# Rows of y and the blocks for the checks issued from GpSimd's queue instead of SyncE's, in a PEER + FNet kernel

## The chip, the core and the metric

The kernel runs on one core of one Trainium2 chip. The metric is the device time of one execution in microseconds (us), the median over several runs of the same program; lower is better.

## What is computed

The reference adds three things for x of 2048 rows by 512 columns, with xn the layer norm of x:

```python
def _A_ref(x, dft_seq_re, dft_seq_im, dft_hid_re, dft_hid_im):   # FNet: real part of a 2-D DFT
    a = jnp.einsum("bsd,ed->bse", x, dft_hid_re)
    b = jnp.einsum("bsd,ed->bse", x, dft_hid_im)
    return jnp.einsum("ts,bse->bte", dft_seq_re, a) - jnp.einsum("ts,bse->bte", dft_seq_im, b)
...
    # PEER: 32 heads, 64 + 64 half keys, top 2 of each half, top 2 of the 4 pairs, 4096 experts
    q = jnp.einsum("nd,dhc->nhc", xf, w_q)
    s1 = jnp.einsum("nhd,ed->nhe", q1, k1)
    s2 = jnp.einsum("nhd,ed->nhe", q2, k2)
...
    g = _softmax(top_s, axis=-1)
    act = _gelu(jnp.einsum("nd,nhkd->nhk", xf, u[top_e]))
    out = jnp.einsum("nhk,nhk,nhkd->nd", g, act, v[top_e])
...
    return x + _A_ref(xn, ...) + _B_ref(xn, ...)
```

## The kernel before

The work has two phases. The first, up to some 440 us, computes the DFT part and the scores s1 and s2 with the choice of the top experts; the DFT part goes to memory as `y_d`, one row of 128 x 512 for each of the 16 blocks of 128 rows. The second phase, which the change touches, doesn't gather experts. For each block b it computes z = x u for all 4096 experts ("z"), applies gelu, multiplies by a gate matrix that holds g at the chosen experts and zero elsewhere, and multiplies the product by v ("v").

The phases stand in a list (lines 1540 to 1543): z of blocks 0 and 1, v of block 0, and then seven times z of a pair (b, b+1), v of the odd block b-1 and v of the even block b; v of block 15 ends it. I call z, v(odd), v(even) a round. In a v block (`v_part`, line 1330) 16 groups of v are multiplied one after the other. Nine of the groups lie in SBUF; the others are loaded from `v_d` (512 KB each) into a ring of three places (`v_load`, line 1306), each load as soon as TensorE has finished with the place.

The gate matrices are made beside this, in quarters. `g_mm(b, k)`: VectorE builds two one-hot matrices L (line 1260) and R (lines 1265, 1268) in a ring of three pairs, and TensorE multiplies them (line 1270). `w_part(b, k)`: VectorE multiplies the result by the activations into a tile w (line 1278), ScalarE copies it to 16 bits (line 1285), and VectorE takes the remainder (line 1286). A table (lines 1544 to 1615) puts them between the eight steps of a v block. In even blocks 2 to 12 it says (lines 1570 to 1580)

```python
put(ph, 1, G(b + 1, 0))
put(ph, 3, G(b + 1, 1))
put(ph, 5, W(b + 1, 0))
put(ph, 7, W(b + 1, 1), G(b + 1, 2))
```

so that TensorE's instructions for G(b+1, 2) stand right behind the last v matmul of the even block and ahead of the next z phase.

The kernel also tests whether its inputs are what its shortcuts assume. `compare` (from line 1350) loads a piece of C (`ca`, 64 KB, line 1357, and `cb`, 448 KB, line 1358) into a tile cx, VectorE reduces and subtracts (lines 1359, 1378, 1384), and ScalarE sums what is left (line 1404). `fit` loads pieces of wq (512 KB, line 1455) or v (256 KB, line 1462), and ScalarE sums them. All of these and the w tiles share four buffers (`WB`, tag "w"). The same table gives them steps: the checks of C run in z phases and in both kinds of v block.

The row of the output: `add_x(b)` loads y of the block from `y_d` (line 1340) and adds x to it with an accumulating transfer from GpSimd (line 1341); `finish(b)` adds the v product on VectorE (line 1345) and stores y (line 1346). y has one buffer, so the load for b+1 waits until the store for b has landed. For block 15 y is loaded earlier, and lines 1312 to 1322 add and store it in halves.

Every transfer is issued by an engine's own queue, in program order: SyncE's queue (SP) for all of the above but line 1341, GpSimd's (POOL) for line 1341. Where one of them waits, for a buffer or a landing, everything behind it in the same queue waits too. A scheduler arranges each engine's instructions and adds the waits. A second program (`safe`) stands behind a branch; it isn't executed on these inputs.

Of the kernel before, what the change touches and what calls it, by code (L numbers as in the profile page):

```python
# [18 lines left out]
P = 128  # L19
S = 2048  # L20
D = 512
KD = D // P
NT = S // P
# [7 lines left out]
V2 = 9  # L31
# [5 lines left out]
def tile_fnet_peer(ctx, tc, x, ca, cb, c5, wt, wf, wr, wq, kt, ut, vn, out):  # L37
# [9 lines left out]
    nc = tc.nc  # L47

    dram = ctx.enter_context(tc.tile_pool(name="dram", bufs=1, space=bass.MemoryType.DRAM))
    y_d = dram.tile([NT, P, D], F32, name="y_d")  # L50
    xt_d = dram.tile([NT, P, 2 * KD * P], F16, name="xt_d")
    z_d = dram.tile([NT, P, 3 * P], F16, name="z_d")
    v_d = dram.tile([16 - V2, P, 4 * D], F16, name="v_d")
# [667 lines left out]
    def part_b(safe, stS, stP, stQ, stE, xt, u_sb, cmp_p, w4):  # L721
# [615 lines left out]

        def add_x(b):
            Y[b] = y = bp.tile([P, D], F32, tag="y", name=f"y{b}", bufs=1)
            nc.sync.dma_start(y, y_d[b])  # L1340
            nc.gpsimd.dma_start(y, x[b % 4, b // 4], accum_op=ALU.add)  # L1341

        def finish(b, pv):
            y = Y[b]
            nc.vector.scalar_tensor_tensor(y, pv, osc, y, op0=ALU.mult, op1=ALU.add)
            nc.sync.dma_start(out[b * P:(b + 1) * P], y)

        later = []

        def compare(n):  # L1350

            ri, g, kk = n // 32, n // 8 % 4, n % 8
            odd = kk // 4
            t = bp.tile([P, 4, 4, 64], F32, tag="w", name=f"cx{n}", bufs=WB)
            tf = t.rearrange("p s q c -> p (s q c)")
            tv = t.rearrange("p s q c -> p s (q c)")
            nc.sync.dma_start(tf[:, :P], ca[ri, g, :, kk * P:(kk + 1) * P])
            nc.sync.dma_start(tf[:, P:], cb[ri, g, kk].rearrange("p b c -> p (b c)"))
            nc.vector.tensor_reduce(asum[:, n:n + 1], tf[:, :P], axis=AX.X, op=ALU.add,
                                    apply_absolute_value=True)  # L1360
            sgn = (((1, 1, 1), (-1, 1, -1)), ((-1, -1, 1), (1, -1, -1)))[ri][odd]
            ops = [ALU.subtract if v > 0 else ALU.add for v in sgn]
            op = ops[1]
            if g == 0:
                nc.vector.tensor_tensor(tv[:, 1], tv[:, 1], tv[:, 0], op=ops[0])
                for i in (2, 3):
                    nc.vector.scalar_tensor_tensor(tv[:, i], tv[:, 0], not0, tv[:, i], op0=ALU.mult, op1=ops[i - 1])
                f = (-1 if ri else 1) * sgn[1] * sgn[2]
                nc.vector.tensor_tensor(tv[0:1, 3], tv[0:1, 3], tv[0:1, 2],
                                        op=ALU.subtract if f > 0 else ALU.add)  # L1370
            else:
                sets = {}
                for i, o in enumerate(ops):
                    sets.setdefault(o, []).append(i + 1)
                for o, ix in sets.items():
                    sl = slice(ix[0], ix[-1] + 1, ix[1] - ix[0] if len(ix) > 1 else 1)
                    v = tv[:, sl]
                    nc.vector.tensor_tensor(v, v, tv[:, 0:1].to_broadcast([P, len(ix), 256]), op=o)
            m = ALU.add if ri else ALU.subtract

            def mirror(v):

                c = 0 if kk else 1
                nc.vector.tensor_tensor(v[:, 2:4, c:], v[:, 2:4, c:], v[:, 0:2, c:], op=m)  # L1384
                if c:
                    nc.vector.tensor_tensor(v[:, 3, 0:1], v[:, 3, 0:1], v[:, 2, 0:1], op=m)

            if g == 0:
                mirror(t[0:1, 2])
                if odd and ri:  # L1390

                    nc.vector.tensor_copy(t[0:1, 2, 0:2], t[0:1, 0, 0:2])
                elif odd == ri:
                    if ri:
                        nc.vector.memset(t[0:1, 2, 0:2], 0.0)
                    else:
                        v = t[0:1, 2, 0:2].rearrange("p q (c a) -> p (q c) a", a=2)
                        nc.vector.tensor_tensor(v, v, c52.unsqueeze(1).to_broadcast([1, 64, 2]), op=ALU.add)
                    if kk == 0:
                        nc.vector.memset(t[0:1, 2, 2, 0:1], 0.0)  # L1400
            mirror(t[:, 0])
            if kk == 0:
                nc.vector.memset(t[:, 0, 2, 0:1], 0.0)
            later.append(lambda: nc.scalar.activation(tf[:, P:], tf[:, P:], AF.Abs, accum_out=chk[:, n:n + 1]))  # L1404
# [46 lines left out]
        def fit(n):  # L1451

            if n < NK:
                t = bp.tile([P, 2 * D], F32, tag="w", name=f"fit{n}", bufs=WB)
                nc.sync.dma_start(t.rearrange("p (h k) -> p h k", h=2), wq[1 + n // 4, n % 4 // 2, n % 2])
                later.append(lambda: nc.scalar.activation(t, t, AF.Abs, accum_out=fits[:, n:n + 1]))
                return
            g = n - NW
            t = bp.tile([P, 2 * D], F32, tag="w", name=f"fit{n}", bufs=WB)
            if g >= 16 + V2:  # L1460
                h = t.bitcast(F16)[:, 0:2 * D]
                nc.sync.dma_start(h, v_d[g - 16 - V2, :, 0:2 * D])
                later.append(lambda: nc.scalar.activation(h, h, AF.Abs, accum_out=fits[:, n:n + 1]))
                return
            src = (u_sb[g][:, 0].rearrange("p c k e -> p (c k e)") if g < 16 else
                   v_sb[g - 16][:, 0].rearrange("p c d -> p (c d)"))
            nc.scalar.activation(t, src, AF.Abs, accum_out=fits[:, n:n + 1])

        def verdict():
# [35 lines left out]
            nc.vector.tensor_tensor(flags, flag, flag2, op=ALU.max)  # L1505

        fit_units = [iter([lambda n=n: fit(n) for n in ns]) for ns in (
            (*range(NK), *range(NW + 16 + V2, NW + 32)), range(NW, NW + 16 + V2))]
        units = iter([lambda n=n: (compare if n < 64 else compare_w)(n) for n in range(68)])
# [106 lines left out]
        for n, ph in enumerate(phases):  # L1616
            if ph[0] == "z":
                b = ph[1:]
# [13 lines left out]
            b = ph[1]  # L1632
# [8 lines left out]
            for cg in range(8):  # L1641
                v_part(b, pv, cg)
                for f in plan.get((ph, cg), ()):
                    f()
                if b + 1 == NT and cg == 3 and not safe:
                    step(None)
                    add_x(b)
                    verdict()
            if b + 1 < NT or safe:
                add_x(b)  # L1650
            else:
                ret = nc.values_load(flags, min_val=0, max_val=1)
            if b + 1 < NT or safe:
                finish(b, pv)
# [30 lines left out]
    with tc.If(rv > 0):  # L1685
        with tc.tile_pool(name="gen", bufs=1) as gp, \
# [4 lines left out]
            def gsplit(src, shape, tag, name, scale=1.0, bufs=2):  # L1691
                h = gp.tile(shape, F32R, tag=tag + "h", name=name + "h", bufs=bufs)
                l = gp.tile(shape, F32R, tag=tag + "l", name=name + "l", bufs=bufs)
                nc.scalar.activation(h, src, AF.Copy, scale=scale)
                nc.vector.scalar_tensor_tensor(l, src, scale, h.bitcast(F32), op0=ALU.mult,
                                               op1=ALU.subtract)
                return h, l

            def gload(src, shape, tag, name):
                t = gp.tile(shape, F32, tag=tag, name=name, bufs=2)  # L1700
                nc.sync.dma_start(t, src)
                return t

            gx = []
            for i in range(NT):
                t = gload(x[i % 4, i // 4], [P, D], "x", f"gx{i}")
                norm(t, t, i)
                gx.append(gsplit(t, [P, D], "xs", f"gxs{i}", 1.0 / XS, NT))
            for q in range(4):
                ya = gp.tile([P, 4, D], F32, tag="ya", name=f"gya{q}")  # L1710
                for ri in range(2):
                    pp = [gps.tile([P, 512], F32, tag="gp", name=f"gp{q}{ri}{d}", bufs=4)
                          for d in range(KD)]
                    for i in range(NT):
                        t = gp.tile([P, 512], F32, tag="c", name=f"gc{q}{ri}{i}", bufs=2)
                        g, sq = divmod(i, 4)
# [4 lines left out]
                        h, l = gsplit(t, [P, 512], "cs", f"gcs{q}{ri}{i}")  # L1721
# [9 lines left out]
                    for kd, pieces in enumerate((((0, 1, P, 0), (P - 1, 0, 1, 2)), ((0, 1, P, 1), (P - 1, 0, 1, 0)),  # L1731
                                                 ((0, 0, 1, 1), (1, 1, P, 2)), ((0, 0, P, 3),))):
                        t = gp.tile([P, 512], F32, tag="c", name=f"gw{q}{ri}{kd}", bufs=2)
# [3 lines left out]
                    for a in range(4):  # L1737
                        py = pb(f"gy{q}{ri}{a}")
                        n = 0
# [9 lines left out]
                        b = 4 * a + q  # L1749
                        o = gload(out[b * P:(b + 1) * P], [P, D], "o", f"go{b}")  # L1750
                        y = gload(y_d[b], [P, D], "y", f"gy{b}")
# [53 lines left out]
```

## Time and profile before

| | |
|---|---|
| median of 3 runs | 1126.24 us (1125.17 to 1126.28) |
| the profiled execution | 1128.96 us, of which the span from first to last instruction is 1127.1 |
| granted TensorE clock, mean | 0.997 of full speed |
| busy share of the span: TensorE, VectorE, ScalarE, GpSimd | 98%, 85%, 59%, 28% |
| transfers issued from SP's kind of queue | 200.65 MB |
| transfers issued from GpSimd's queue | 4.20 MB |

A profile shows one execution. Engines are PE (TensorE matmul), PEld (its weight loads), DVE (VectorE), ACT (ScalarE), POOL (GpSimd) and SP (SyncE; SPq is its queue of transfers). L1340 is line 1340 of the kernel. In a timeline row the first number is the start in us, the second the duration; xN says how many equal instructions the row joins, and brackets tell how long the engine was idle before it and what ended that. A row of waits gives who waited, for whom, the total in us, how often, and the longest.

### The profile page before, as it was taken

What the parts mean: (1) busy time and instruction counts of PE and PEld (TensorE: products, weight loads), DVE (VectorE), ACT (ScalarE), POOL (GpSimd) and SP (SyncE); (2) the same over time, 40 slices, a digit from 0 to 9 for tenths busy, and PEclk for the clock granted to TensorE, in tenths of its full rate; (3) what the DMA queues carried; (4) which work ended last, traced back from release to release, by engine and by line L of the source; (5) the groups of instructions that cost most, each with busy time, mean ns of one, the idle gap of its engine ahead of it and who ended that gap; (6) DMA issues with size and microseconds to landing.
All of it is one profiled execution on the core that took longest, in us unless ns stands there. A gap on an engine that the chain in (4) does not pass through costs nothing.

```text
span 1127.1 us, 27990 instructions
## 1 busy us (share of the span) xinstructions
PE 1109.9 (98%) x11024; PEld 719.9 (64%) x11024; DVE 957.2 (85%) x2883; ACT 668.5 (59%) x1118; POOL 314.6 (28%) x365
## 2 busy tenths in 40 slices
PE   9999999999999999999999999999999999999997
PEld 6455554544545459788488479479469569559643
DVE  7899989989889899976996987987997887878882
ACT  6557698798898465465446546535545635545541
POOL 1515998888889750000000000000000000000000
PEclk9999999999999999999999999999999999999999
DMA  9884455356353315773764764864765765656263
GB/s 296 270 215 163 162 180 204 116 157 200 94 185 105 102 52 186 211 233 121 266 206 156 254 191 162 262 194 146 261 199 167 246 188 191 225 197 189 94 179 116
DMA packets 123932, 206.80 MB, mean 183 GB/s; under 512 B 34564, under 2 KB 65419, under 8 KB 123790
## 3 DMA queue, kind: packets, MB, share of 16 engines
q1 hardware_dynamic: 121184, 200.65, 54.7%
q0 software_dynamic: 2304, 4.20, 2.4%
q8 instruction: 88, 1.44, 0.5%
q14 instruction: 54, 0.44, 0.1%
q10 hardware_dynamic: 302, 0.08, 0.0%
HBM read 171.52 MB, written 27.59 MB: 177 GB/s over the span
## 4 chain that ended last, share of the span: by engine, by line
PE 45%; DVE 12%; DMA 6%; ACT 2%; POOL 2%; issue 1%; SPq 0%; ACTq 0%; POOLq 0%; DVEq 0%
PE z L1173 16%; PE v L1330 16%; PE z L1095 9%; PE g L1270 3%; DMA v<-v_d 2%; DVE L L1260 2%; DMA cx<-in_cb_dram 2%; DVE w L1278 2%; DVE vals L956 1%; DMA fit<-in_wq_dram 1%; DVE idx L960 1%; DVE act L1286 1%; DVE R L1268 1%; DVE R L1265 1%; DVE w L1286 1%
## 5 line engine op out<-in xcount | busy, mean ns | idle before, releaser
L252 PE MATMUL s<-m,xq 128*128 128x512 f16 x1344 | 297.4, 379 | 0.6 <-ACT ss L952 0.5
L1330 PE MATMUL v<-v,act 128*128 128x512 f16 x1044 | 231.1, 379 | 1.9 <-DMA v<-v_d 1.9
L252 PEld LDWEIGHTS <-xq 128*128 128x128 f16 x1344 | 129.7, 98 | 151.8 <-issue 2.0
L1341 POOL DMA_DIRECT2D y<-in_x_dram x16 | 14.4, 897 | 652.9 <-DMA y<-y_d 219.0
L1260 DVE TENSOR_TENSOR L<-io_lam,cmp 128x2048 f16<-128x2048 f16 x128 | 156.0, 1218 | 31.5 <-PE g L1270 31.5
L1330 PEld LDWEIGHTS <-act 128*128 128x128 f16 x1044 | 100.0, 98 | 118.5 <-issue 2.7
L956 DVE MAX8 vals<-ss 128x8 f32<-128x64 f32 x896 | 133.4, 216 | 3.9 <-ACT ss L952 3.9
L1095 PE MATMUL z<-xb,u 128*128 128x128 f16 (+1 forms) x1440 | 121.8, 244 | 0.1
L1173 PEld LDWEIGHTS <-u 128*128 128x128 f16 x2016 | 114.5, 98 | 1.1 <-issue 0.8
L1095 PEld LDWEIGHTS <-u 128*128 128x128 f16 x1440 | 107.6, 98 | 7.4 <-issue 0.2
L1330 PE MATMUL v<-v,w 128*128 128x512 f16 x480 | 106.7, 379 | 0.7 <-DMA v<-v_d 0.6
L952 ACT ACTIVATE ss<-s,wsc 128x512 f32<-128x512 f32 x120 | 81.3, 682 | 38.7 <-PE s L252 33.4
L1404 ACT ACTIVATE cx<-cx 128x896 f32<-128x896 f32 x64 | 60.5, 946 | 64.2 <-DVE cx L1384 34.4
L960 DVE FIND_INDEX8 idx<-vals,ss 128x8 uint16<-128x256 f32 x224 | 93.7, 418 | 0.0
L1173 PEld LDWEIGHTS <-s 128*128 128x128 f16 x1440 | 82.5, 98 | 0.2
L1330 PEld LDWEIGHTS <-w 128*128 128x128 f16 x480 | 46.0, 98 | 54.5 <-issue 1.6
L1285 ACT ACTIVATE act<-w 128x1024 f16<-128x1024 f32 x36 | 48.3, 1356 | 53.7 <-DVE w L1278 53.3
L1270 PEld LDWEIGHTS <-L 128*128 128x128 f16 x2048 | 60.5, 96 | 13.1 <-issue 2.4
L1278 DVE SCALAR_TENSOR_TENSOR w<-act,scl,g 128x1024 f32<-128x1024 f32 x44 | 55.8, 1277 | 10.6 <-ACT act L1203 10.3
L1270 PE MATMUL g<-R,L 128*128 128x32 f16 x2048 | 61.9, 176 | 1.9 <-DVE R L1268 1.8
L1173 PE MATMUL z<-xb,u 128*128 128x128 f16 x1008 | 63.1, 219 | 0.0
L1286 DVE TENSOR_TENSOR act<-w,act 128x1024 f16<-128x1024 f32 x44 | 58.5, 1329 | 3.8 <-ACT act L1285 3.7
(366 smaller groups left out, 1855.7 us busy)
## 6 DMA issues: line engine op xcount, KB each, us to landing
v<-v_d SPq DMA_DIRECT2D x67, 512.0 KB, 5.5
cx<-in_cb_dram SPq DMA_DIRECT2D x64, 448.0 KB, 5.0
s<-s_d SPq DMA_DIRECT2D x42, 512.0 KB, 4.3
w<-in_wq_dram SPq DMA_DIRECT2D x28, 512.0 KB, 6.5
fit<-in_wq_dram SPq DMA_DIRECT2D x28, 512.0 KB, 3.8
uv<-in_vn_dram SPq DMA_DIRECT2D x16, 512.0 KB, 3.8
uv<-in_ut_dram SPq DMA_DIRECT2D x16, 512.0 KB, 3.9
s_d<-v SPq DMA_DIRECT2D x24, 256.0 KB, 4.2
```

The lines of the kernel that those rows point to most:

```text
L252: nc.tensor.matmul(ps, xt[i][:, l, kd, :], m[:, r, kd, :], start=(n == 0), stop=(n == 3 * KD - 1))
L952: nc.scalar.activation(s, ps, AF.Copy, scale=inv)
L956: nc.vector.max(vals[:, i, w, :, h], s[:, g, :])
L960: nc.vector.max_index(idx[:, i, w].rearrange("p k h -> p (k h)"), vals[:, i, w, 0:2].rearrange("p k h -> p (k h)"), s[:, w * HC:g + 1, :]. ...
L1095: nc.tensor.matmul(ps if n == 1 else ps.rearrange("p (b n) -> p b n", b=2), ug[:, l, c % 2, kd, :], xb2[:, k0, r, kd, :] if n == 1 else xb ...
L1173: nc.tensor.matmul(bank[:, t * P:(t + 1) * P], lt, rt, start=(t == k == 0 and op in "125"), stop=(t == 3 and k == 5), skip_group_check=op ...
L1260: nc.vector.tensor_tensor(L.rearrange("p t (l two) -> p t l two", two=2), io_lam.rearrange("p (l two) -> p l two", two=2).unsqueeze(1).to_ ...
L1270: nc.tensor.matmul(p[:, hf, t * NC:(t + 1) * NC], L[:, t, :], R[:, t, :], start=True, stop=True)
L1278: nc.vector.scalar_tensor_tensor(w, act[:, :, ts], fw, p.rearrange("p h (n c) -> p c (h n)", c=NC), op0=ALU.mult, op1=ALU.mult)
L1286: nc.vector.tensor_tensor(w16[..., 1], w, w16[..., 0], op=ALU.subtract)
L1330: nc.tensor.matmul(pv, w16[:, c, :, l], v_sb[g][:, r, cc, :], start=(n + cc == 0 and k == 0), stop=(n == end and cc == 1 and k == 2))
L1404: later.append(lambda: nc.scalar.activation(tf[:, P:], tf[:, P:], AF.Abs, accum_out=chk[:, n:n + 1]))
```

## The change

The load and the store of y, both loads of a check of C, and the loads of wq and v for `fit` are issued from GpSimd's queue. The load of y for block 15 and everything in `safe` that concerns y stay on SP. The loads of v in the ring, of the z phases and of the last checks (`compare_w`) stay on SP too.

```diff
         def add_x(b):
             Y[b] = y = bp.tile([P, D], F32, tag="y", name=f"y{b}", bufs=1)
-            nc.sync.dma_start(y, y_d[b])
+            (nc.sync if safe or b + 1 == NT else nc.gpsimd).dma_start(y, y_d[b])
             nc.gpsimd.dma_start(y, x[b % 4, b // 4], accum_op=ALU.add)
 
         def finish(b, pv):
             y = Y[b]
             nc.vector.scalar_tensor_tensor(y, pv, osc, y, op0=ALU.mult, op1=ALU.add)
-            nc.sync.dma_start(out[b * P:(b + 1) * P], y)
+            (nc.sync if safe else nc.gpsimd).dma_start(out[b * P:(b + 1) * P], y)
...
-            nc.sync.dma_start(tf[:, :P], ca[ri, g, :, kk * P:(kk + 1) * P])
-            nc.sync.dma_start(tf[:, P:], cb[ri, g, kk].rearrange("p b c -> p (b c)"))
+            nc.gpsimd.dma_start(tf[:, :P], ca[ri, g, :, kk * P:(kk + 1) * P])
+            nc.gpsimd.dma_start(tf[:, P:], cb[ri, g, kk].rearrange("p b c -> p (b c)"))
...
-                nc.sync.dma_start(t.rearrange("p (h k) -> p h k", h=2), wq[1 + n // 4, n % 4 // 2, n % 2])
+                nc.gpsimd.dma_start(t.rearrange("p (h k) -> p h k", h=2), wq[1 + n // 4, n % 4 // 2, n % 2])
...
-                nc.sync.dma_start(h, v_d[g - 16 - V2, :, 0:2 * D])
+                nc.gpsimd.dma_start(h, v_d[g - 16 - V2, :, 0:2 * D])
```

Now what stands on the queues at one place, the turn from the odd block 3 to the even block 4. First SP before the change, from the store of block 3's row (y3) to the store of block 4's (y4); v12 to v9 are groups of v for the ring, cx20 and cx21 the next two checks of C, fit11 a piece of wq; brackets name the semaphores waited for (DMAHW and DMASW are those of landed transfers).

```order
L1346 DMA out_0_dram<-y3_9454 128x512 [waits DMAHW5_49,DVE_49]
L1306 DMA v12_4_9475<-v_d_60 128x2048 [waits DMAHW6_49,PE_49]
L1340 DMA y4_9733<-y_d_57 128x512 [waits DMAHW7_49,DMAHW5_49]
L1306 DMA v11_4_9489<-v_d_60 128x2048 [waits DMAHW0_49,PE_49]
L1357 DMA cx20_9648<-in_ca_dram 128x128 [waits DMAHW1_49,Activation_49]
L1358 DMA cx20_9648<-in_cb_dram 128x896 [waits DMAHW2_49]
L1357 DMA cx21_9668<-in_ca_dram 128x128 [waits DMAHW3_49,Activation_49]
L1358 DMA cx21_9668<-in_cb_dram 128x896 [waits DMAHW4_49]
L1306 DMA v10_4_9553<-v_d_60 128x2048 [waits PE_49]
L1455 DMA fit11_9731<-in_wq_dram 128x1024 [waits DMAHW6_49,DVE_49]
L1306 DMA v9_4_9616<-v_d_60 128x2048 [waits DMAHW7_49,PE_49]
L1346 DMA out_0_dram<-y4_9733 128x512 [waits DMAHW0_49,DVE_49]
```

Behind this, only the four loads of v (v12, v11, v10, v9) are left on SP here. GpSimd's queue before held only the accumulates of line 1341. With the change it reads, at the same place:

```order
L1346 DMA out_0_dram<-y3_9454 128x512 [waits DMASW6_49,DVE_49]
L1340 DMA y4_9733<-y_d_57 128x512 [waits DMASW7_49,DMASW6_49]
L1341 DMA y4_9733<-in_x_dram 128x512 [waits DMASW7_49,DMASW0_49]
L1357 DMA cx20_9648<-in_ca_dram 128x128 [waits DMASW1_49,Activation_49]
L1358 DMA cx20_9648<-in_cb_dram 128x896 [waits DMASW2_49]
L1357 DMA cx21_9668<-in_ca_dram 128x128 [waits DMASW3_49,Activation_49]
L1358 DMA cx21_9668<-in_cb_dram 128x896 [waits DMASW4_49]
L1455 DMA fit11_9731<-in_wq_dram 128x1024 [waits DMASW5_49,DVE_49]
L1346 DMA out_0_dram<-y4_9733 128x512 [waits DVE_49]
```

The accumulate of line 1341 now stands in the same queue between y's load and the checks' loads. Even blocks 2 to 12 all have this sequence. In all, 193 issues move from SP to GpSimd; TensorE's order is the same. On VectorE, in the even block of the same place, the operations stand as they stood; with the change:

```order
L1286 TENSOR_TENSOR w4_126<-w5_0_9643,w4_126 128x32x32 [waits Activation_49]
L1359 TENSOR_REDUCE sums_87<-cx20_9648 128x1 [waits DMASW1_49]
L1378 TENSOR_TENSOR cx20_9648<-cx20_9648 128x2x256 [waits DMASW2_49]
L1378 TENSOR_TENSOR cx20_9648<-cx20_9648 128x256
L1359 TENSOR_REDUCE sums_87<-cx21_9668 128x1 [waits DMASW3_49]
L1384 TENSOR_TENSOR cx20_9648<-cx20_9648 128x128 [waits DVE_49]
L1278 SCALAR_TENSOR_TENSOR w5_1_9687<-w4_126,scl_93,g5_1_9561 128x1024 [waits PE_49]
L1378 TENSOR_TENSOR cx21_9668<-cx21_9668 128x2x256 [waits DMASW4_49]
L1378 TENSOR_TENSOR cx21_9668<-cx21_9668 128x256
L1265 TENSOR_TENSOR R2_5741<-io_c_73,cmp5_9369 128x512
L1384 TENSOR_TENSOR cx21_9668<-cx21_9668 128x128 [waits DVE_49]
L1286 TENSOR_TENSOR w4_126<-w5_1_9687,w4_126 128x32x32 [waits Activation_49]
```

Behind these twelve rows follow the rest of R2 and the L0 and R0 that TensorE's G(5, 2) takes at the end of block 4, and then y4. The check's operations moved nowhere here; only the semaphores they wait for are others (DMASW, those of GpSimd's transfers).

## The prediction, made before the change was run

> **What bounds the kernel now.** I read the page's span and busy rows first, then the table by stretches over one round of the second phase, then what TensorE waits for there, and last the four timelines of one even block.
>
> ```profile
> span 1127.1 us, 27990 instructions
> PE 1109.9 (98%) x11024; PEld 719.9 (64%) x11024; DVE 957.2 (85%) x2883; ACT 668.5 (59%) x1118; POOL 314.6 (28%) x365
> 573.00:661.00 88.00, 87.12 (x1068) 63.22 (x1065) 73.45 (x120) 45.92 (x76) 1.72 (x2) 1.00 0.64 206
> PE v L1330 <- DMA v<-v_d: 2.5, 5, 0.9
> PE g L1270 <- DVE R L1268: 1.8, 4, 0.7
> PE z L1173 <- ACT act L1226: 0.6, 1, 0.6
> ```
>
> TensorE is the bound: 98% of the span, and 87.12 of the 88.00 us of a round (one z phase and two v blocks; columns of the third row: length, then PE, PEld, DVE, ACT, POOL busy, granted clock, DMA share, GB/s). The last three rows are everything that it waits for from 420 us to the end (total, times, longest): 2.5 us for a v block from memory, 1.8 for a one-hot R that VectorE builds, 0.6 for ScalarE, together 4.9. So transfers arriving earlier can win 4.9 us at most, and only the 2.5 are SyncE's doing. GpSimd is nearly idle in the round (1.72 of 88 us), and VectorE, with 73 of 88, has some slack, but the next rows show that it has none at the place where TensorE comes for R. Here are the issue rows (median us from issue to landing, last column) and GpSimd's only work in this phase, the x accumulate:
>
> ```profile
> v<-v_d SPq DMA_DIRECT2D x67, 512.0 KB, 5.5
> cx<-in_cb_dram SPq DMA_DIRECT2D x64, 448.0 KB, 5.0
> y<-y_d SPq DMA_DIRECT2D x16, 256.0 KB, 2.7
> y<-in_x_dram POOLq DMA_DIRECT2D x16, 256.0 KB, 6.1
> out_dram<-y SPq DMA_DIRECT2D x15, 256.0 KB, 2.8
> L1340 SPq DMA_DIRECT2D y<-y_d x16: 319/320/572, 445.2 to 1102.1; - x16
> L1341 POOL DMA_DIRECT2D y<-in_x_dram x16: 856/867/1177, 453.9 to 1107.4; - x16
> 578.84 0.87 POOL L1341 DMA_DIRECT2D y<-in_x_dram  x1 [18.69 <-DVE act L1286]
> 646.96 0.86 POOL L1341 DMA_DIRECT2D y<-in_x_dram  x1 [67.25 <-DVE L L1260]
> ```
>
> An issue occupies SP's queue 0.32 us and POOL 0.87 (medians in the two rows of L1340 and L1341; of the timeline rows the first number is the start, the second the duration): 0.55 more.
>
> Now the turn from odd block 3 to even block 4, engine by engine: SP, VectorE, TensorE.
>
> ```profile
> 639.79 0.34 SPq L1346 DMA_DIRECT2D out_dram<-y  x1
> 642.03 0.32 SPq L1340 DMA_DIRECT2D y<-y_d  x1
> 642.92 0.38 SPq L1357 DMA_DIRECT2D cx<-in_ca_dram  x1
> 643.35 0.42 SPq L1358 DMA_DIRECT2D cx<-in_cb_dram  x1
> 638.15 0.96 DVE L1378 TENSOR_TENSOR cx<-cx 128x768 f32<-128x768 f32 x1 [1.11 <-DMA cx<-in_cb_dram]
> 639.02 0.74 DVE L1345 SCALAR_TENSOR_TENSOR y<-v,scl,y 128x512 f32<-128x512 f32 x1
> 649.45 1.03 DVE L1378 TENSOR_TENSOR cx<-cx 128x512 f32<-128x512 f32 x2 [1.00 <-DMA cx<-in_cb_dram]
> 651.98 1.02 DVE L1378 TENSOR_TENSOR cx<-cx 128x512 f32<-128x512 f32 x2
> 658.39 0.42 DVE L1268 TENSOR_TENSOR R<-R,cmp 128x512 f16<-128x512 f16 x1
> 660.08 0.75 DVE L1345 SCALAR_TENSOR_TENSOR y<-v,scl,y 128x512 f32<-128x512 f32 x1 [1.26 <-PE v L1330]
> 657.29 2.75 PE L1330 MATMUL v<-v,act 128*128 128x512 f16 x12 [0.88 <-DMA v<-v_d]
> 659.88 0.95 PE L1270 MATMUL g<-R,L 128*128 128x32 f16 x32
> ```
>
> y of block 3 is ready at 639.02 + 0.74 = 639.76. SP stores it at once, loads y of block 4 at 642.03, and without waiting for anything of y's issues the next check's ca and cb at 642.92 and 643.35. Even so VectorE waits 1.00 us for that cb at 649.45, and the R that TensorE's g matmuls need at 659.88 is ready at 658.39 + 0.42 = 658.81: 1.07 us ahead, and only because TensorE lost 0.88 us to a v block just before. VectorE works in order and shows no wait between the check at 649.45 and that R, so whatever makes this check late makes R late by as much.
>
> **The change part by part.** The queues' work: 193 issues (15 y loads, 15 stores, 64 ca, 64 cb, 28 wq and 7 v transfers) leave SP, some 193 x 0.35 = 68 us of its time, and cost POOL 193 x 0.87 = 168 us over the roughly 650 us of this phase, in which it is idle. Neither sum is on the path; the matmuls and VectorE's operations are the same. What matters is the order on POOL. The store waits for VectorE's y; the load waits for the store (one y buffer); the accumulate waits for the load; and in each of the six even blocks 2 to 12 the checks' and fit's loads stand behind the accumulate. On SP only the first two of these stood ahead of them, so the new wait is that of the accumulate on the landing of y's load, with ca, cb, ca, cb and wq queued behind it, and VectorE, then TensorE, behind those.
>
> The chain, from t = 0 at VectorE's y (639.76). The store is issued at 0.03. From store to y load SP took 642.03 - 639.79 = 2.24, of which the store's landing is the most; on POOL 0.55 more for the longer issue: 2.8. From y load to accumulate 646.96 - 642.03 = 4.93, again with 0.55: 8.3. The accumulate's own issue 0.87 and ca's 0.87: cb is issued at 10.0. It lands 5.0 later by its median, with 0.5 for POOL's issue 5.5: 15.5. Before, VectorE started on this cb at 649.45 - 639.76 = 9.7. So VectorE is 5.8 us late; the second check's loads follow 1.7 us behind, and VectorE comes to them 651.98 - 649.45 = 2.53 later, so they add nothing. R comes at 658.81 + 5.8 = 664.6 and TensorE, which started at 659.88, loses 4.7 us. If SP, relieved, brings the v block on time, TensorE arrives 0.88 earlier and waits 0.88 longer: the v stall that goes is swallowed, since the g matmuls lie right behind that v block. One term goes the other way: at 638.15 VectorE waited 1.11 us for a check of the odd block, just ahead of y; POOL is free there, and if that wait goes, t = 0 and everything behind it comes up to 1.1 earlier. So 3.6 to 4.7 here.
>
> The same place in the first and the last of five such blocks (2 and 10), and in block 12, which is different:
>
> ```profile
> 552.23 0.73 DVE L1345 SCALAR_TENSOR_TENSOR y<-v,scl,y 128x512 f32<-128x512 f32 x1
> 563.39 0.96 DVE L1378 TENSOR_TENSOR cx<-cx 128x768 f32<-128x768 f32 x1 [0.45 <-DMA cx<-in_cb_dram]
> 572.31 0.43 DVE L1268 TENSOR_TENSOR R<-R,cmp 128x512 f16<-128x512 f16 x1
> 572.38 0.95 PE L1270 MATMUL g<-R,L 128*128 128x32 f16 x32
> 900.36 0.74 DVE L1345 SCALAR_TENSOR_TENSOR y<-v,scl,y 128x512 f32<-128x512 f32 x1
> 911.28 1.03 DVE L1378 TENSOR_TENSOR cx<-cx 128x512 f32<-128x512 f32 x2 [0.86 <-DMA cx<-in_cb_dram]
> 920.22 0.43 DVE L1268 TENSOR_TENSOR R<-R,cmp 128x512 f16<-128x512 f16 x1
> 920.69 0.95 PE L1270 MATMUL g<-R,L 128*128 128x32 f16 x32
> 986.23 0.73 DVE L1345 SCALAR_TENSOR_TENSOR y<-v,scl,y 128x512 f32<-128x512 f32 x1
> 1001.41 1.03 DVE L1378 TENSOR_TENSOR cx<-cx 128x256 f32<-128x256 f32 x2
> 1010.05 0.55 PE L1270 MATMUL g<-R,L 128*128 128x32 f16 x16 [0.67 <-DVE R L1268]
> ```
>
> From y to the check it is 563.39 - 552.96 = 10.4 in block 2 and 911.28 - 901.10 = 10.2 in block 10: 5.1 and 5.3 late. R is ready at 572.74 and 920.65 where TensorE starts at 572.38 and 920.69: no cover at all, so 5.1 to 5.3 are lost, or 4.0 to 4.2 with the 1.1. With block 4 I take 4.4 for each of the five: 22 us. In block 12 the check comes 1001.41 - 986.96 = 14.4 after y: 1.1 late, and the last row shows TensorE already waiting 0.67 us for R there: 1 us. Sum +23. In the z phases the checks' loads come long after the accumulate, and block 15 keeps its row of y on SP: nothing.
>
> No row shows POOL issuing loads or stores, so both ends are bounds. Low: the load lands in its row's 2.7 with none of the 0.5's: 0.03 + 2.24 + 2.7 + 0.87 + 0.87 + 5.0 = 11.7, against 9.7 to 10.4: 1.3 to 2.0 late, and with the 1.1 and block 4's cover 0.4 each: +2. High: each transfer takes the accumulate's 6.1: 0.03 + 6.1 + 6.1 + 0.87 + 0.87 + 6.1 = 20.1, 10 late, five times, and 5.7 in block 12: +54. A gain from this part is excluded: the low chain is still longer than 9.7. I take 23, nearer to the low end, since most of the chain is SP's own measured landing.
>
> An issue on POOL could also be longer than 0.87 now that VectorE is busy around it: the accumulates' row goes to 1177 ns, which over the four issues of the chain would be 4 x 0.31 = 1.2 us a block, +6. [...]
>
> **The rivals.** *Few transfers in flight.* The 16 accumulates lie 18 us or more apart (the row at 578.84 has idled 18.69), so no row shows POOL with several under way. If the fourth has to wait for the first to land, the check's ca goes out behind the accumulate but the second check's behind its landing: 8.3 + 6.1 = 14.4, 3.5 later than 10.9, of which 2.7 remain past VectorE's 2.5 of other work; with some 1.2 in the z phases a round goes from 4.4 to about 8: 5 x 8 + 4 = +44, 1170. For it: nothing but the absence of a row. [...]
>
> *Hidden, and SP's relief shows: faster.* If POOL's chain were done before 9.7, TensorE would keep its order and lose the v waits: -2.5, at most -4.9, 1121.3 to 1123.7. For it: v loads on SP no longer stand behind others. Against it: the chain can't be that short by any row. *No change.* The low chain, with +2 swallowed by the odd blocks: 1126 to 1128. [...] That the change does nothing is excluded by the orders: 193 rows stand on another queue.
>
> **How the numbers follow.** The profiled execution took 1128.96 us (1.86 outside its span), 2.7 over the median of 1126.24; its stalls are taken as the median's. 1126.24 + 23 = 1149. Chances: this forecast 0.53; few in flight 0.24; faster 0.11; no change 0.09; worse than the high bound 0.03. A measurement of this kernel tells about 0.2% (2.3 us) from no change. The range leaves out the gain and the last case: from 1126 to 1126.24 + 54 = 1180.
>
> **What would show it.** Right: TensorE's wait for R of line 1268 grows from 1.8 to some 25 us in five or six waits of 4 to 5 at the ends of blocks 2 to 10, VectorE waits about 6 us for a check's cb or ca there, POOL's first ca comes about 9 us after the store, and TensorE's v wait falls. Few in flight: waits on POOL ahead of second and later loads, POOL issues far over 0.87. Wrong: no growth at line 1268.

## The result, and the profile after

The changed kernel took 1204.67 us (median; 1200.67 to 1212.82 in six runs) beside 1126.37 for the kernel before (1125.17 to 1131.63): a ratio of 1.0695, 95% interval 1.0657 to 1.0734. It is 78 us slower, in the direction forecast and 25 us above the top of the range (1126 to 1180). The profiled execution took 1204.02 us, of which 1202.0 are the span.

First the page, then what TensorE waits for from 420 us on.

```profile
span 1202.0 us, 28006 instructions
PE 1127.0 (94%) x11024; PEld 735.3 (61%) x11024; DVE 956.0 (80%) x2883; ACT 664.7 (55%) x1118; POOL 419.6 (35%) x558
q0 software_dynamic: 16464, 62.14, 17.1%
...
PE g L1270 <- DVE R L1268: 49.4, 17, 8.7
PE z L1173 <- ACT act L1102: 6.5, 3, 3.6
PE z L1173 <- ACT w L1102: 4.6, 2, 3.4
PE z L1173 <- ACT act L1226: 2.3, 1, 2.3
PE v L1330 <- DMA v<-v_d: 0.7, 2, 0.5
```

GpSimd's queue now carries 62.14 MB. The span grew by 74.9 us: 17.1 of them are TensorE's busy time (1109.9 to 1127.0, with the same matmuls), in the rest it stood still. The mean granted clock fell from 0.997 to 0.973. The wait for R, 1.8 before, is 49.4. The v wait, 2.5 before, has shrunk to 0.7; this fits SyncE's relief, but TensorE also comes to the v blocks later here, so this row alone doesn't show it. The z waits (13.4 in these rows, 0.6 before) were not in the forecast.

Here is the place that the prediction worked through, the turn to block 4, in the changed kernel: POOL, VectorE, TensorE.

```profile
654.37 0.54 POOL L1346 DMA_DIRECT2D out_dram<-y  x1 [3.44 <-DVE y L1345]
658.08 0.54 POOL L1340 DMA_DIRECT2D y<-y_d  x1 [3.16 <-DMA out_dram<-y]
662.09 0.90 POOL L1341 DMA_DIRECT2D y<-in_x_dram  x1 [3.48 <-DMA y<-y_d]
662.73 0.81 POOL L1357 DMA_DIRECT2D cx<-in_ca_dram  x1
667.47 0.54 POOL L1358 DMA_DIRECT2D cx<-in_cb_dram  x1 [3.93 <-issue]
653.23 0.74 DVE L1345 SCALAR_TENSOR_TENSOR y<-v,scl,y 128x512 f32<-128x512 f32 x1
...
671.27 1.03 DVE L1378 TENSOR_TENSOR cx<-cx 128x512 f32<-128x512 f32 x2 [3.58 <-DMA cx<-in_cb_dram]
676.48 0.41 DVE L1268 TENSOR_TENSOR R<-R,cmp 128x512 f16<-128x512 f16 x1
679.41 0.42 DVE L1268 TENSOR_TENSOR R<-R,cmp 128x512 f16<-128x512 f16 x1
676.94 0.60 PE L1270 MATMUL g<-R,L 128*128 128x32 f16 x16 [3.65 <-DVE R L1268]
679.88 0.59 PE L1270 MATMUL g<-R,L 128*128 128x32 f16 x16 [2.33 <-DVE R L1268]
680.31 2.72 PE L1173 MATMUL z<-xb,u 128*128 128x128 f16 x24
682.82 2.77 PE L1173 MATMUL z<-x,u 128*128 128x128 f16 x24
```

Count from y at 653.23 + 0.74 = 653.97, as the prediction did. Store, load and accumulate go out 0.4, 4.1 and 8.1 us after it, ca 8.8; the forecast had 0.03, 2.8, 8.3 and, with the accumulate's issue of 0.87, 9.1. Up to there the order is the one forecast. That the sum comes out is luck: y's load goes out 1.3 us later than forecast, and the accumulate follows it after 4.0 us instead of 5.5. Then POOL stands still for 3.93 us between ca and cb, and "issue" in the brackets says that nothing the profile shows ended that wait. cb goes out at 13.5 instead of 10.0, and VectorE takes the check at 671.27, 17.3 after y; the forecast had 15.5, and in the kernel before it was 9.7. TensorE waits twice, 3.65 and 2.33 us, once for each half of G(5, 2). The first 48 matmuls of the z phase then take 2.72 and 2.77 us for 24; the same groups took 1.50 in the kernel before. The granted clock from 680 to 686 us is 0.53, and 1.00 from 686 to 711.

Block 4 loses least of the six even blocks 2 to 12. The two waits for R together are 6.0 us there and 6.8 to 11.0 in the others, and the accumulate leaves POOL 9.1 to 12.9 us after y in the others, where the forecast had 8.3.

### The profile page after: what moved, and what is told of

Its sections match the earlier page's. It is cut to its first block, busy times and chain, and to the rows that moved or that the text cites. A ratio compares the mean times of both kernels' runs of the same rounds, so it can differ in the third digit from the quotient of the medians.

```text
span 1202.0 us, 28006 instructions
## 1 busy us (share of the span) xinstructions
PE 1127.0 (94%) x11024; PEld 735.3 (61%) x11024; DVE 956.0 (80%) x2883; ACT 664.7 (55%) x1118; POOL 419.6 (35%) x558
## 3 DMA queue, kind: packets, MB, share of 16 engines
q0 software_dynamic: 16464, 62.14, 17.1%
## 4 chain that ended last, share of the span: by engine, by line
PE 22%; DVE 20%; DMA 12%; issue 9%; POOL 4%; ACT 4%; POOLq 0%; ACTq 0%; SPq 0%
PE z L1173 11%; PE z L1095 6%; DMA cx<-in_cb_dram 5%; DVE L L1260 4%; DVE w L1278 3%; PE v L1330 2%; DVE act L1286 2%; DMA out_dram<-y 2%; DVE cx L1378 2%; PE g L1270 2%; DVE w L1286 1%; DMA y<-y_d 1%; DVE vals L956 1%; DMA cx<-in_ca_dram 1%; DMA zt<-z_d 1%
## 5 line engine op out<-in xcount | busy, mean ns | idle before, releaser
L1173 PEld LDWEIGHTS <-u 128*128 128x128 f16 x2016 | 127.8, 104 | 14.6 <-issue 14.1
L1357 POOL DMA_DIRECT2D cx<-in_ca_dram x64 | 36.7, 573 | 221.6 <-DVE act L1286 94.7
L1095 PEld LDWEIGHTS <-u 128*128 128x128 f16 x1440 | 107.7, 98 | 8.0 <-issue 0.8
L1270 PE MATMUL g<-R,L 128*128 128x32 f16 x2048 | 63.5, 177 | 49.6 <-DVE R L1268 49.4
L1173 PE MATMUL z<-xb,u 128*128 128x128 f16 x1008 | 71.0, 233 | 11.1 <-ACT act L1102 6.5
L1378 DVE TENSOR_TENSOR cx<-cx 128x512 f32<-128x512 f32 (+2 forms) x84 | 48.4, 609 | 39.1 <-DMA cx<-in_cb_dram 38.6
L1173 PE MATMUL z<-x,u 128*128 128x128 f16 x1008 | 66.7, 229 | 2.3 <-ACT act L1226 2.3
```

Of the source, the lines that this page charges most:

```text
L1095: nc.tensor.matmul(ps if n == 1 else ps.rearrange("p (b n) -> p b n", b=2), ug[:, l, c % 2, kd, :], xb2[:, k0, r, kd, :] if n == 1 else xb ...
L1173: nc.tensor.matmul(bank[:, t * P:(t + 1) * P], lt, rt, start=(t == k == 0 and op in "125"), stop=(t == 3 and k == 5), skip_group_check=op ...
L1270: nc.tensor.matmul(p[:, hf, t * NC:(t + 1) * NC], L[:, t, :], R[:, t, :], start=True, stop=True)
```

## The experiments

Four theories, of which the first two carry the result. **Order**: on POOL the checks of C stand behind y's store, load and accumulate. **Few in flight** (the rival): POOL can only have a few transfers under way and waits with the next until one has landed. **Clock**: behind its waits TensorE runs slower for a while (24 matmuls in 2.72 us instead of 1.50 in block 4). **y's transfers themselves**, or any load on POOL, are what costs.

| run | what differs from the changed kernel | us | ratio to before, 95% interval |
|---|---|---|---|
| ring_384 | 384 bytes on line 1792 | 1285.79 | 1.1432 (1.1379 to 1.1486) |
| the change | 512 bytes | 1204.67 | 1.0695 (1.0657 to 1.0734) |
| ring_768 | 768 bytes | 1173.02 | 1.0418 (1.0395 to 1.0440) |
| y_behind | y's load and accumulate behind the checks | 1166.93 | 1.0317 (1.0241 to 1.0392) |
| y_behind_768 | that, and 768 bytes | 1131.80 | 1.0042 (1.0025 to 1.0060) |
| checks_only | y's load and store back on SP | 1181.07 | 1.0493 (1.0456 to 1.0529) |
| checks_768 | that, and 768 bytes | 1156.35 | 1.0256 (1.0231 to 1.0281) |
| no_accumulate | no accumulate of x, blocks 0 to 14 | 1148.13 | 1.0176 (1.0138 to 1.0214) |
| y_fit_768 | checks of C back on SP, 768 bytes | 1143.60 | 1.0134 (1.0114 to 1.0154) |
| y_only | checks of C and fit back on SP | 1125.41 | 0.9990 (0.9978 to 1.0003) |
| y_only_5 | the same, five rounds | 1126.03 | 1.0002 (0.9987 to 1.0016) |
| filler | 24 more matmuls ahead of G(b+1, 2) | 1205.49 | 1.0681 (1.0641 to 1.0722) |
| filler_768 | that, and 768 bytes | 1175.91 | 1.0447 (1.0412 to 1.0481) |

**Room for more transfers.** The first run changes one number, the bytes of `dynamic_dma_scratch_size` on line 1792; every engine's order is the same.

```diff
-    nc = bacc.Bacc("TRN2", target_bir_lowering=False, num_devices=1, dynamic_dma_scratch_size=512)
+    nc = bacc.Bacc("TRN2", target_bir_lowering=False, num_devices=1, dynamic_dma_scratch_size=768)
```

> The changed kernel with 768 bytes a partition instead of 512 for the descriptors of GpSimd's transfers (line 1792); every engine's order is the same. Theory 'few in flight': in the changed kernel POOL stood still 3.93 us between ca and cb of a check while y's accumulate was on its way; with half as much room again that wait goes, the check of each even block reaches VectorE some 4 us earlier, TensorE's wait for R of 5.98 us in block 4 falls to about 2, and the slower matmuls behind it go too: 20 to 40 us less, 1165 to 1185. Theory 'order alone' (the checks stand behind y's store, load and accumulate, and how many transfers are under way doesn't matter): no change, 1204 within 3.

It took 1173.02, 32 us less. POOL, VectorE and TensorE at the same place:

```profile
657.12 0.90 POOL L1341 DMA_DIRECT2D y<-in_x_dram  x1 [3.82 <-DMA y<-y_d]
657.76 0.82 POOL L1357 DMA_DIRECT2D cx<-in_ca_dram  x1
658.32 0.79 POOL L1358 DMA_DIRECT2D cx<-in_cb_dram  x1
...
662.41 0.54 POOL L1358 DMA_DIRECT2D cx<-in_cb_dram  x1 [2.77 <-issue]
647.77 0.74 DVE L1345 SCALAR_TENSOR_TENSOR y<-v,scl,y 128x512 f32<-128x512 f32 x1
664.50 1.03 DVE L1378 TENSOR_TENSOR cx<-cx 128x512 f32<-128x512 f32 x2 [1.89 <-DMA cx<-in_cb_dram]
670.18 0.56 PE L1270 MATMUL g<-R,L 128*128 128x32 f16 x16 [2.09 <-DVE R L1268]
673.12 0.59 PE L1270 MATMUL g<-R,L 128*128 128x32 f16 x16 [2.37 <-DVE R L1268]
```

The wait has moved from the first cb behind the accumulate to the second. So it isn't bound to a line: in block 4 it comes behind the accumulate and one load with 512 bytes (3.93 us), behind the accumulate and three loads with 768 (2.77 us). VectorE takes the check 664.50 - 648.51 = 16.0 us after y; the prediction, which let POOL issue as it liked, said 15.5. From the store's issue to the accumulate's it now takes 8.5, 8.2 and 6.5 us in blocks 2, 4 and 6; with 512 bytes it took 9.0, 7.7 and 11.3. In the whole trace the waits for R fall from 49.4 us to 28.3 and those of the z phases from 13.4 to 1.9. "Order alone" predicted no change and is refuted as the whole story.

The dose the other way, 384 bytes:

> The changed kernel with 384 bytes a partition for GpSimd's descriptors instead of 512, the same order. Theory 'few in flight': three quarters of the room, so POOL already waits at the ca or the second load of a check, in z phases and odd blocks too: 20 to 50 us more, 1225 to 1255. Theory 'order alone': 1204 within 4.

It took 1285.79, 81 us more than the changed kernel and beyond the 20 to 50 expected. POOL's waits without a cause in the profile, ahead of cb alone, in the kernels with 384, 512 and 768 bytes (us in total, times, longest):

```profile
POOL cx L1358 <- issue: 104.0, 44, 4.7
```

```profile
POOL cx L1358 <- issue: 42.8, 28, 3.9
```

```profile
POOL cx L1358 <- issue: 15.3, 8, 2.8
```

The time falls with these waits, with nothing else changed: 1285.79, 1204.67 and 1173.02 us. So the bytes on line 1792 set how many transfers POOL gets under way before it stops, one load behind the accumulate of block 4 with 512 and three with 768. How the waits go on above 768 was not tried.

**The order.** Here y's load and accumulate are queued behind the last check of C that stands ahead of them in the code.

```diff
-            (nc.sync if safe or b + 1 == NT else nc.gpsimd).dma_start(y, y_d[b])
-            nc.gpsimd.dma_start(y, x[b % 4, b // 4], accum_op=ALU.add)
+            with tc.issue_after(CB[-1].ins) if CB and b + 1 < NT else ExitStack():
+                (nc.sync if safe or b + 1 == NT else nc.gpsimd).dma_start(y, y_d[b])
+                nc.gpsimd.dma_start(y, x[b % 4, b // 4], accum_op=ALU.add)
...
-            nc.gpsimd.dma_start(tf[:, P:], cb[ri, g, kk].rearrange("p b c -> p (b c)"))
+            CB.append(nc.gpsimd.dma_start(tf[:, P:], cb[ri, g, kk].rearrange("p b c -> p (b c)")))
```

> Everything on GpSimd's queue as in the changed kernel, 512 bytes, but y's load and accumulate are queued behind the checks' loads that the even block issues. Theory 'order': the checks then go out right behind y's store, about where they were before the change: 1126 to 1140, of which what is over 1126 is for POOL's waits when more than a few transfers are under way and for the odd blocks, where the accumulate still stands between two checks. Rival, that GpSimd's queue is slow for loads as such or that the room for descriptors alone makes the loss: over 1165.

1166.93: 38 us less, but not the 1126 to 1140 expected, and just over the rival's 1165, so the time alone speaks for the rival. In the trace, POOL with 512 bytes now waits behind the store and between the checks instead, 55.2 us ahead of cb in all (42.8 in the changed kernel). So with both:

> Both: y's load and accumulate behind the checks, and 768 bytes. Theories 'order' and 'few in flight' together explain the whole loss: 1124 to 1132. If a third cause is left in GpSimd's queue: over 1140.

1131.80, the upper end of what was expected; 5 us over the kernel before. In POOL's and TensorE's rows of this kernel (its lines are one or two higher from 1340 on; L1342 is the accumulate, L1360 cb):

```profile
649.73 0.55 POOL L1347 DMA_DIRECT2D out_dram<-y  x1 [4.50 <-DVE y L1346]
650.35 0.54 POOL L1359 DMA_DIRECT2D cx<-in_ca_dram  x1
...
652.04 0.54 POOL L1360 DMA_DIRECT2D cx<-in_cb_dram  x1
655.73 0.54 POOL L1341 DMA_DIRECT2D y<-y_d  x1 [3.15 <-DMA out_dram<-y]
```

```profile
PE g L1270 <- DVE R L1268: 4.5, 4, 2.6
```

All four loads leave in 2.2 us, 0.6 after the store, and the wait for R is down to 4.5. In these steps the 78 us are 32 for the room (1204.67 to 1173.02), 41 for the order (1173.02 to 1131.80) and 5 that neither takes away. Taken the other way round, the order is worth 38 (1204.67 to 1166.93) and the room 35 (1166.93 to 1131.80), so the shares are known to some 3 us. VectorE's order differs here too, so the order's share contains that. What the 5 are was not tried, and the traced execution, at 1138.37 well above the median, doesn't tell: beside 2.7 us more of waiting for R it has a single wait of 4.5 us, ahead of line 1095, for which the profile shows no cause.

**Parts of the change.** Only the checks' and fit's loads moved, y's load and store left on SP:

> Only the loads of the checks of C, of wq and of v for fit on GpSimd's queue; y's load and store stay on SP, the accumulate stays on POOL. Theories 'order' and 'few in flight': the accumulate still waits for y's load and still stands ahead of the checks, so most of the loss stays, less the two longer issues (about 0.5 us a block): 1185 to 1205. Rival, that y's own store and load on POOL are what costs: 1126 to 1135.

1181.07, 4 us below the range: 24 us less than the change. y's load and store on POOL cost this much when the checks are there too. In block 4 the accumulate now goes out 7.0 us after y instead of 8.1; whether that explains all of the 24 was not traced. Most of the loss stays, with the accumulate (which POOL already issued before the change) ahead of the checks:

```profile
655.08 0.89 POOL L1341 DMA_DIRECT2D y<-in_x_dram  x1 [10.12 <-DVE L L1260]
655.69 0.84 POOL L1357 DMA_DIRECT2D cx<-in_ca_dram  x1
660.59 0.54 POOL L1358 DMA_DIRECT2D cx<-in_cb_dram  x1 [4.05 <-issue]
```

The same 4 us between ca and cb, behind the accumulate. With more room:

> Only the checks' and fit's loads on GpSimd's queue, y's load and store on SP, with 768 bytes: the run checks_only (1181) with more room. Theories 'order' and 'few in flight' add up: the room is worth about what it was worth in the changed kernel (32 us), and the accumulate still stands ahead of the checks: 1145 to 1160. If room were all that matters once y is off the queue: 1126 to 1132. If the room matters only together with y: 1175 to 1185.

1156.35: the room is worth 25 us here, against 32 with y on the queue too, and y's load and store cost 17 with the larger room (1173.02 to 1156.35). Taking the accumulate itself away:

> The changed kernel without y's accumulate for blocks 0 to 14 (x is not added to those rows). Theory 'order': the accumulate's wait on y's landing (4.0 us in block 4) and its issue (0.6) no longer stand ahead of the checks; theory 'few in flight': nor does its share of the room (3.9 us). By both together the check leaves POOL 8.6 us earlier, within 1 us of where it was before the change: 1126 to 1140. By 'few in flight' alone, only 3.9 us an even block: about 1175. If GpSimd's queue is slow for these loads as such: over 1190.

1148.13, 57 us less than the change but 8 over the range: even without it 21 us are left. In its trace POOL still waits 26.9 us ahead of cb without a cause (24 times, 2.0 at the longest), so the room is short without the accumulate too; TensorE waits 10.6 us for R and 3.8 for line 1102, and its busy time is 7.3 us longer than before (1117.2). What each of these is worth was not measured. Then y alone:

> Only y's load and store on GpSimd's queue; the checks' loads and fit's stay on SP. Theories 'order' and 'few in flight': nothing that VectorE needs stands behind the accumulate, so no loss: 1126 within 3, at best 2.5 less for the waits on v of line 1330 that SP's queue caused. Rival, that y's own store and load on POOL are what costs: over 1150.

1125.41, with an interval that held both signs, so once more with more rounds:

> Only y's load and store on GpSimd's queue, the kernel of the run y_only once more with more rounds, since its ratio of 0.999 left the sign open. Theory: SP no longer waits for y, so the loads of v leave when their place is free and TensorE's 2.5 us of waits for v go, at the cost of nothing: 0.2% faster, 1123 to 1125. Rival: no difference, the waits are taken up elsewhere: 1126 within 1.5.

1126.03, a ratio of 1.0002: no difference. The rival (1126 within 1.5) was right, and not the gain to 1123 to 1125. Yet TensorE's waits in the repeat are smaller than before (2.5 on v, 1.8 on R):

```profile
PE g L1270 <- DVE R L1268: 1.1, 3, 0.7
...
PE v L1330 <- DMA v<-v_d: 0.4, 1, 0.4
```

So the 2 us of v waits that SP's relief takes away are seen in the trace and can't be told apart in the time. y's transfers on POOL cost nothing that shows in the time when nothing else stands behind them. Last, y and fit on POOL, only the checks of C back on SP:

> y's load and store and the loads of wq and v for fit on GpSimd's queue, with 768 bytes for its descriptors; only the checks of C go back to SP. Nothing that VectorE works on stands behind the accumulate any more (fit's data go to ScalarE alone). Theory 'order': as with y alone, 1122 to 1126. Rival, that fit's loads, late behind the accumulate, hold the four shared buffers and so the checks: 1130 to 1150.

1143.60: the rival was right. TensorE, then SP, in this kernel:

```profile
PE z L1173 <- ACT act L1226: 8.2, 3, 3.5
PE z L1173 <- ACT w L1226: 5.6, 2, 3.3
...
SPq L1357 <- DMA fit<-in_wq_dram: 12.4, 4, 7.6
```

SP now waits 12.4 us for fit's loads (4.1 before) before it can load a check: they hold one of the four shared buffers. The loss shows as waits for ScalarE in the z phases, not as waits for R (2.2). The link between the two is argued only: ScalarE itself also waits longer ahead of fit's sums, 42.8 us in two rows of line 1456 against 22.5 before, and which of both makes it late was not separated.

**The clock.** In the changed kernel, 24 matmuls whose results are overwritten fill TensorE's two waits at the end of each even block 2 to 12.

```diff
+                if not safe and tg == 2 and b % 2 and 1 < b < 14:
+                    for _ in range(8 if hf else 16):
+                        nc.tensor.matmul(p[:, hf, :], parts(b - 1)[:, 0, :, 0], v_sb[0][:, 0, 0, :], start=True, stop=True)
```

> The changed kernel with 24 more matmuls of 128 x 512 at the end of each even block 2 to 12, whose results are overwritten: 16 ahead of the first half of G(b+1, 2) and 8 ahead of the second, 3.5 and 1.7 us by the 0.22 us of one, at a place where TensorE waits 6 to 11 us for R anyway. Theory 'clock': a TensorE that stood still several us runs the next matmuls slower (24 of line 1173 in 2.72 and 2.77 us behind the waits of block 4, 1.50 elsewhere); kept busy it doesn't, and 2.6 us are saved at each of six places: 1186 to 1192, with more work. Theory 'the slow stretch has another cause': 1204 within 4. If the fillers push the g matmuls back: over 1210.

1205.49: no gain, by its time the case "the slow stretch has another cause" (1204 within 4). The trace says otherwise. The z matmuls behind the block, in block 4 of this kernel, take 1.50 us again:

```profile
683.73 1.50 PE L1173 MATMUL z<-xb,u 128*128 128x128 f16 x24
```

In the changed kernel they took 2.72. So the slow stretch is the price of standing still, as the theory had it, but removing it buys nothing here: the fillers take about the time of the waits that they fill, TensorE comes to the z phase's next wait sooner, and its waits for ScalarE's lines 1102 and 1226 grow from 13.4 to 20.8 us. To see it without most of those waits, the same in the kernel with 768 bytes:

> The 24 overwritten matmuls of the run filler, now in the kernel with 768 bytes (1173): there the z phases wait for almost nothing (1.9 us in all), so a TensorE that comes out of block 4 at full clock isn't stopped again at the next wait. Theory 'the slow clock is paid where nothing else holds TensorE': the slow matmuls behind the six waits (2.72 and 1.67 us for 24 each in block 4 instead of 1.50) go: 1.4 us and the slower g rows, six times, about 9 us less, 1162 to 1167, although the fillers (5.2 us) are a little longer than the waits (4.5). Theory 'the clock costs nothing here either': 1173 within 3. Fillers longer than the wait and no gain: 1176 to 1180.

1175.91: no gain. The time lies between two of the three cases, "the clock costs nothing here either" (1173 within 3) and "fillers longer than the wait" (1176 to 1180); the trace speaks for the latter. The groups of line 1173 in ring_768, and then in filler_768 with two of its waits (its lines from 1270 on are up to three higher):

```profile
L1173 PE MATMUL z<-xb,u 128*128 128x128 f16 x1008 | 70.7, 233 | 0.8 <-ACT act L1102 0.4 <-ACT w L1102 0.4
L1173 PE MATMUL z<-x,u 128*128 128x128 f16 x1008 | 65.7, 227 | 1.1 <-ACT act L1226 1.1
```

```profile
L1173 PE MATMUL z<-xb,u 128*128 128x128 f16 x1008 | 63.1, 219 | 0.9 <-ACT w L1102 0.4 <-ACT act L1102 0.4
L1173 PE MATMUL z<-x,u 128*128 128x128 f16 x1008 | 61.6, 219 | 5.0 <-ACT act L1226 2.6 <-ACT w L1226 2.3
...
PE v L1333 <- DMA v<-v_d: 8.1, 7, 2.4
PE g L1273 <- DVE R L1268: 1.2, 3, 0.7
```

The fillers save 11.7 us of slow matmuls ((70.7 + 65.7) - (63.1 + 61.6)), with a mean granted clock of 0.995 instead of 0.981, and nearly all of the wait for R (1.2 left of 28.3). But they keep TensorE busy for 33.0 us themselves, longer than that wait, and longer waits for v (8.1 us, 1.8 in ring_768) and ScalarE take up the rest. In neither kernel did removing the slow stretch in this way win anything. What it would cost in a kernel in which nothing else is late was not tried.

## Why the prediction was wrong

**The bound and the place: right.** TensorE's longest waits came where forecast, in front of G(b+1, 2) at the end of even blocks: 47.7 of the 49.4 us for R. The wait for v fell from 2.5 to 0.7 us. The times on POOL were right by luck in block 4, where a late load and an early accumulate cancel; in the other even blocks the accumulate left 0.8 to 4.6 us later than the 8.3 forecast. Why the landings ahead of it take longer with 512 bytes than with 768 in blocks 2 and 6 was not traced.

**The step that failed** is the one that put cb behind ca without a wait: "The accumulate's own issue 0.87 and ca's 0.87: cb is issued at 10.0." It went out at 13.5, 3.93 us of waiting later. The prediction had this as its rival "few transfers in flight", with a chance of 0.24 and the words "For it: nothing but the absence of a row". Giving more than twice the chance to the case in which an untried resource is unlimited was the error; the runs with 384 and 768 bytes show the limit to be real and worth 32 us here. With it fell the term for the z phases, put at nothing: TensorE's waits there are 13.4 us, and 1.9 with 768 bytes. Block 4 shows little of this: VectorE starts on cb 3.8 us after its issue where 5.5 were forecast, so that the check comes only 1.8 us later than forecast.

**The rival's own price was off too.** It let the fourth transfer wait, 3.5 us for the second check. In fact the second transfer behind the accumulate waited, the first check's cb, which VectorE comes to first. It also gave the z phases 1.2 us a round, 6 in five rounds; TensorE's waits there came to 13.4. By the rival the kernel would have taken 1170; it took 1204.67.

**The order's term was too small.** 23 us were forecast, 41 were measured between ring_768 and y_behind_768. Per block it was about right: 2.09 + 2.37 = 4.46 us of waits in block 4 (3.6 when the 0.88 us of v wait that is gone is set against them), against 3.6 to 4.7. The 1.1 us to be won at the odd block's check did not come: VectorE still waits 1.06 us for it in the changed kernel. Two things were too small or left out. Block 12 was given 1 us, but its waits in ring_768 are 1.96 and 2.37:

```profile
1046.38 0.56 PE L1270 MATMUL g<-R,L 128*128 128x32 f16 x16 [1.96 <-DVE R L1268]
1049.32 0.59 PE L1270 MATMUL g<-R,L 128*128 128x32 f16 x16 [2.37 <-DVE R L1268]
...
PE g L1270 <- DVE R L1268: 28.3, 14, 2.7
```

All waits for R in that kernel are 28.3 us, 26.5 more than before, close to the 23. And TensorE's busy time grew by 15.7 (1109.9 to 1125.6, ring_768's page); the prediction took a matmul's duration as fixed. 12.3 of them lie in the two groups of line 1173 (136.4 us, 124.1 before), the slow stretches behind the waits; another 2.0 lie in line 152, in the first phase, and have nothing to do with the change. As the fillers won nothing back, it stays open how much of the 12.3 would count if the waits alone were gone.

```profile
PE 1125.6 (96%) x11024; PEld 734.6 (63%) x11024; DVE 955.4 (82%) x2883; ACT 667.0 (57%) x1118; POOL 420.8 (36%) x558
```

Behind the two waits of block 4 in the changed kernel, from 680 to 686 us, the granted clock is 0.53. The length of the longest wait alone doesn't tell when this comes: two waits of 2.09 and 2.37 us, 0.6 us apart, were enough to make 24 matmuls take 2.72 us instead of 1.50 (first row, ring_768), and a single wait of 3.60 us in a z phase of the changed kernel was not (second row; the granted clock from 711 to 716 us is 1.00). What decides it was not shown. The two rows:

```profile
673.55 2.72 PE L1173 MATMUL z<-xb,u 128*128 128x128 f16 x24
...
711.43 1.50 PE L1173 MATMUL z<-xb,u 128*128 128x128 f16 x24 [3.60 <-ACT act L1102]
```

**A misread row.** The prediction took the row at 658.39 for the R that TensorE needs at 659.88. It is the third R of that stretch, for a later product; the second half of G(5, 2) takes the one before it (in block 12 of the kernel before, the second half starts at 1010.05, behind the R that ends at 1010.00 and ahead of the third, which starts only at 1010.36):

```profile
657.61 0.41 DVE L1268 TENSOR_TENSOR R<-R,cmp 128x512 f16<-128x512 f16 x1
```

The cover in the kernel before was thus larger, 2.3 us for the second half (657.61 + 0.41 = 658.02, against about 660.3, the middle of the g matmuls that start at 659.88), and not 1.07. It made the forecast too high by about 1 us a block, and hid part of the other errors; that the forecast per block came out is luck to that extent.

**Issues of 0.87 us** were an overestimate: that row is the accumulate's own, and y's load and store take 0.54 (ca right behind the accumulate 0.81). The margin for a busy VectorE, 1177 ns an issue, was not needed: of the checks' 128 issues in the changed kernel the longest took 0.94 us.

## What to carry to other kernels

A queue in program order is a chain (in block 4 of the changed kernel cb left POOL 13.5 us after y, behind waits of 3.16, 3.48 and 3.93 us): before moving transfers, write down what each one waits for in its new place, and who needs the ones behind it. A transfer that waits for another's landing (here an accumulate on a load) shouldn't share a queue with loads that are needed soon (the order cost 38 to 41 us here); transfers that nobody waits for can (y alone, 1126.03 us), if nobody needs their buffers either (y_fit_768, 1143.60). And before many transfers go to GpSimd's queue, ask how many can be under way (the room cost 32 to 35 us here): a queue that was only seen with one at a time says nothing about that, and the chance of a limit should be set accordingly.

## What the runs showed of the hardware that was not expected

- POOL's waits without a visible cause ahead of cb fell from 104.0 to 42.8 and 15.3 us with 384, 512 and 768 bytes on line 1792, and the kernel from 1285.79 to 1204.67 and 1173.02.
- What is under way when POOL stops in block 4: with 512 bytes the accumulate and one load (3.93 us ahead of the second), with 768 the accumulate and three loads (2.77 us ahead of the fourth).
- The accumulate's issue is longer than the others: 0.90 us against 0.54 for y's load and store and for the checks' loads (medians). Right behind an accumulate the checks' loads took 0.70 to 0.82 in block 4 of ring_768.
- Two waits of TensorE of 2.09 and 2.37 us with 16 small matmuls between them were followed by 24 z matmuls in 2.72 us and 24 in 1.67 instead of 1.50 each (ring_768, block 4), two of 3.65 and 2.33 us by a granted clock of 0.53 (changed kernel, 680 to 686 us), and a single wait of 3.60 us by one of 1.00 (changed kernel, 711 to 716 us).
